# An order written out by hand, products shared between two engines: polysketch attention with a tanh-shrink FFN on Trainium2

## The chip, the cores and the metric

The kernel runs on one core of one Trainium2 chip. The metric is device time in microseconds (us); before the change it is 114.84, the median of three runs (113.99 to 115.63). A core has five engines with a queue each, and each queue runs in its own order: TensorE (PE in the profile; PEld are its weight loads), VectorE (DVE), ScalarE (ACT), GpSimd (POOL) and SyncE (SP), which here only issues DMAs. Queues wait for one another by semaphores.

## The reference

Four batches of four heads, 1088 tokens, head size 32, sketch size r = 8. All inputs and the output are float32.

```python
def phi(x):                                   # 32 -> 8 x 8 = 64 features
    a = np.einsum('rd,bhsd->bhsr', S1, x)
    b = np.einsum('rd,bhsd->bhsr', S2, x)
    return np.einsum('bhsi,bhsj->bhsij', a, b).reshape(*x.shape[:-1], r * r)
q_p, k_p = phi(q), phi(k)
kv  = np.einsum('bhsf,bhsd->bhfd', k_p, v)
z   = np.sum(k_p, axis=2)
num = np.einsum('bhsf,bhfd->bhsd', q_p, kv)
den = np.einsum('bhsf,bhf->bhs', q_p, z)[..., None] + 1e-06
x   = num / den                               # heads side by side: 4352 tokens x 128
h   = x @ w_in                                # 128 -> 2048
out = (h - np.tanh(h)) @ w_out                # 2048 -> 128
```

## The kernel before

**Attention, per batch.** k is transposed on VectorE (`kT`, L583), sketched with S1 and S2 on TensorE (`ksk`, L599, L610), and the sketches are transposed back (`abk`, L616). Three outer products of 768 elements on VectorE make the 64 features of the keys (`w`, L659). TensorE multiplies them with v in 128x32 tiles (L671, `kvmm`). The denominator goes another way: the 8x8 Gram matrix of the two sketches (L638), copied (`gm`, L642), times S2 (L625, `scmm`) gives a third 8-column sketch, so that the product of a query's first and third sketch, summed, is the denominator. The copied kv matrix is transposed (L703) and copied (`kvb`). The queries are transposed (`qT`, L592), sketched in 32x32 tiles (L724), transposed back (`abc`, L729); then VectorE does m = first times third sketch (L741), its sum (L744), 1/den (L747), the first sketch times 1/den (`ap`, L749; called aq in op names), outer products of up to 768 elements (`qp`, L767) and their transposes (`qpT`, L772). The numerator (`num`, L783) is 16 small tiles at a time, 32x32, over the blocks of 128 tokens of a piece. Two casts per piece put it as bf16 into `xT` (L375). A batch has 9 blocks (the last one is half full). Batch 0 is done in pieces of blocks 0 to 2, 2 to 5, 5 to 9; batch 1 in 0 to 5 and 5 to 9; batches 2 and 3 whole.

**FFN.** The 4352 columns of `xT` are taken in ten groups: 256, 384, 448, six of 512, 192. Each has 16 tiles: h = w_in tile times xT (L877), th = -tanh(h) (L881, ScalarE, bf16) and the sum over tiles of w_out tile times th (L892). What is missing, h itself through w_out, comes as two correction matmuls with the product w_in w_out, split into a bf16 high and low part `wch`, `wcl` (L896), over all columns of the group. That product is made on the chip from transposed weights (L845, L855). h lies in one of three PSUM banks; the last three groups, when attention has left its four banks, take pairs of banks and one tanh for 1024 columns. There are 20 tanh tiles of 512 columns. A group ends with a transpose (`ot`, L901) and four stores by SP (eight where a group spans two batches, L911).

**What sets the order.** The kernel makes a list of operations with their reads and writes and with durations and a key; `schedule` runs through them with these durations and appends to each engine's queue the ready operation that can start first, by key within a short window. It also chooses the buffer of each value, and puts filler matmuls (L435: 256 columns of zeros) on TensorE where the plan has it empty in the start. `sync` then sets the semaphores that the dependences need, `emit` issues each queue. GpSimd does memsets, masks and some weight casts; all two-input products but one (`s2r`, L559) are VectorE's. A load waits until at most 1.4 MB of loads are under way. All of k, q, v and the weights are loaded by SP, in order of the keys.

Of the kernel before, what the change touches and what calls it, by code (L numbers as in the profile page):

```python
# [18 lines left out]
GCOLS = [256, 384, 448] + [512] * 6 + [192]  # L19
T_FIRST = 12500.0  # L20
PERIOD = 8900.0
FILL = (214.0, 60.0)
CAP = 1.4e6
PAIRS = 7
URGENT = (-60500.0, 450.0)
PIECES = {0: [(0, 2), (2, 5), (5, 9)], 1: [(0, 5), (5, 9)], 2: [(0, 9)], 3: [(0, 9)]}
OFF = [[0, 9], [17, 26]]
WINDOW = {"tensor": 60.0, "vector": 150.0, "scalar": 60.0, "gpsimd": 30.0, "sync": 30.0}


class _Bank:
    __slots__ = ("t", "ops")

    def __init__(self):
        self.t, self.ops = 0.0, []
# [51 lines left out]
class _Op:  # L87
    __slots__ = ("engs", "fn", "key", "deps", "users", "nleft", "vals", "eng", "lat", "mode",
                 "t0", "t1", "seq", "known", "waits", "inc", "cnt", "sem", "dma", "name", "filler")


class _Prog:
    SWITCH = 125.0
# [4 lines left out]
    def add(self, engs, fn, r=(), w=(), key=0.0, chain=None, dma=0, name="", after=(), mode=None):  # L98
        o = _Op()
        o.engs = engs  # L100
        o.fn, o.key, o.dma, o.name, o.mode = fn, key, dma, name, mode
        o.deps, o.users, o.vals = {}, [], []
        o.filler = False
# [31 lines left out]
    @staticmethod  # L135
    def pick(grp, t):
        best = None
        for c in grp.pool.choices:
            a = 0.0
            for bank in c[0]:  # L140
                if bank.t is None:
                    break
                a = max(a, bank.t)
            else:
                if a <= t and grp.pool.psum:
                    return t, c
                if best is None or a < best[0]:
                    best = (a, c)
        return best and (max(t, best[0]), best[1])

    def schedule(self, filler=None):
        for o in self.ops:
            o.nleft = len(o.deps)
            for d in o.deps:
                d.users.append(o)
            o.t1 = None
        ready = [o for o in self.ops if o.nleft == 0]
        free = {"tensor": 1100.0, "vector": 900.0, "scalar": 900.0, "gpsimd": 900.0, "sync": 700.0}
        self.order = {e: [] for e in free}
        wire = 0.0  # L160
        pemode = None
        fills = True

        def start_of(o, e):
            t = free[e]
            for d, raw in o.deps.items():
                if d.eng == e and not d.dma and e == "tensor":
                    continue
                if d.eng == e and not d.dma:
                    if raw:  # L170
                        t = max(t, d.t1 + d.lat - 45.0)
                    continue
                t = max(t, d.t1 + (0.0 if d.dma else d.lat))
            for v in o.vals:
                if v.grp is not None and v.grp.ap is None:
                    best = self.pick(v.grp, t)
                    if best is None:
                        return None
                    t = best[0]
            return t  # L180

        n = 0
        while n < len(self.ops):
            best = None
            for e in free:
                cands = []
                for o in ready:
                    if e in o.engs:
                        t = start_of(o, e)
                        if t is not None:  # L190
                            cands.append((t, o))
                if not cands:
                    continue
                t0 = min(t for t, _ in cands)
                t, o = min(((t, o) for t, o in cands if t <= t0 + (URGENT[1] if o.key < URGENT[0] and not o.dma else WINDOW[e])), key=lambda x: (x[1].key, x[0]))
                rank = (t, o.key, o.engs[e][0])
                if best is None or rank < best[0]:
                    best = (rank, t, o, e)
            assert best is not None, "stuck"
            _, t, o, e = best  # L200
            for v in o.vals:
                g = v.grp
                if g is not None:
                    if g.ap is None:
                        _, c = self.pick(g, t)
                        g.ap = c[1]
                        m = len(c[0]) // len(g.vals)
                        for u in g.vals:
                            u.banks = c[0][u.index * m:(u.index + 1) * m]
                            u._ap = c[1][u.index]  # L210
                            u.first_deps = [d for bank in u.banks for d in bank.ops]
                            for bank in u.banks:
                                bank.t = None
                    if o in v.phases[0][2]:
                        for d in v.first_deps:
                            o.deps.setdefault(d, d.eng == e and d.seq == len(self.order[e]) - 1)
            if e == "tensor":
                if o.name == "o0.0":
                    fills = False
# [771 lines left out]
```

## Time and profile before

| what | value |
|---|---|
| median of three runs | 114.84 us |
| span of the profiled execution | 112.6 us |
| profiled execution's own time | not listed; the median lies 2.2 us over the span |
| PE busy, instructions | 100.3 us, 1467 |
| DVE busy | 72.1 us, 115 |
| ACT busy | 79.9 us, 164 |
| POOL busy | 5.6 us, 25 |
| first FFN matmul (L877) starts | 19.7 us |
| last output transpose (L901) starts | 108.9 us |
| HBM read, written | 8.81 MB, 2.23 MB |

Busy time is the time in which an engine has an instruction running. Matmuls are pipelined and their ends are modelled, so a row's length (0.38 us for 512 columns) is not what it holds the queue for; the distance from one start to the next is (0.2155 us). A busy PE can still have short holes. The chain is followed back from the last instruction: at each step to what released it. Times in the timeline are from the start of the span.

### The profile page before, as it was taken

The numbers are of one execution on the slowest core, as the hardware profiler recorded it, in microseconds if no ns is written. First come the engines' busy times: TensorE is split into PE (matmuls) and PEld (weight loads), VectorE is DVE, ScalarE is ACT, GpSimd is POOL, SyncE is SP. The second block draws the span as 40 slices with busy tenths as digits, with TensorE's granted clock in tenths as the row PEclk, the third lists the DMA queues.
The fourth block names the chain that finished last, engine by engine and source line by source line (L and its number), as shares of the span: only waits on it lengthen the run. The fifth ranks groups of instructions, "written<-read, shape, count | busy, mean of one in ns | idle before, by whom it ended". The sixth has DMA issues, their size and how long they took to land.

```text
span 112.6 us, 3409 instructions
## 1 busy us (share of the span) xinstructions
PE 100.3 (89%) x1467; PEld 48.7 (43%) x1477; DVE 72.1 (64%) x115; ACT 79.9 (71%) x164; POOL 5.6 (5%) x25
## 2 busy tenths in 40 slices
PE   6975996998799989979999999979999999999960
PEld 4523783455355444436443346334243334334540
DVE  4469374899999999999999992499950020020030
ACT  2101247876487798586599867798969999999950
POOL 5202016000000000000000000000000000000000
PEclk9999999999999999999999999999999999999999
DMA  1999878799987804022000230005004106005035
GB/s 21 259 245 329 255 232 234 243 241 272 226 270 218 165 5 69 0 47 46 0 6 0 44 49 6 6 11 83 0 6 68 25 0 93 0 12 77 4 55 73
DMA packets 25037, 11.24 MB, mean 100 GB/s; under 512 B 18880, under 2 KB 23616, under 8 KB 25024
## 3 DMA queue, kind: packets, MB, share of 16 engines
q1 hardware_dynamic: 24320, 10.97, 40.7%
q8 instruction: 11, 0.18, 0.7%
q10 hardware_dynamic: 704, 0.08, 0.5%
q14 instruction: 2, 0.02, 0.1%
HBM read 8.81 MB, written 2.23 MB: 98 GB/s over the span
## 4 chain that ended last, share of the span: by engine, by line
PE 36%; ACT 28%; DVE 16%; DMA 13%; issue 2%; SPq 1%; DVEq 0%
ACT th L881 25%; PE psb L892 11%; PE psb L877 10%; DMA qL<-in_q_dram 5%; DMA wo_f<-in_moe_w_out_dram 5%; PE psb L783 5%; DVE qp L767 4%; DVE qpT L772 4%; DVE abc L729 3%; DMA kL<-in_k_dram 3%; PE psb L724 3%; PE psb L671 3%; DVE ot L901 2%; PE psb L610 2%; ACT wiT L375 2%
## 5 line engine op out<-in xcount | busy, mean ns | idle before, releaser
L881 ACT ACTIVATE th<-psb 128x512 bf16<-128x512 f32 (+4 forms) x136 | 69.5, 624 | 7.4 <-PE psb L877 6.6
L877 PE MATMUL psb<-xT,wi 128*128 128x512 bf16 (+4 forms) x155 | 50.1, 349 | 1.5 <-DVE xT L375 0.5
L892 PE MATMUL psb<-th,wo 128*128 128x512 bf16 (+4 forms) x157 | 48.2, 348 | 1.4 <-DVE ot L901 0.6
L877 PEld LDWEIGHTS psb<-xT,wi 128*128 128x128 bf16 x160 | 14.9, 97 | 25.3 <-ACT th L881 14.4
L892 PEld LDWEIGHTS psb<-th,wo 128*128 128x128 bf16 x160 | 14.6, 97 | 15.7 <-ACT th L881 7.5
L901 DVE STREAM_TRANSPOSE ot<-psb 128x512 f32<-128x512 f32 (+4 forms) x10 | 6.3, 626 | 22.6 <-PE psb L892 22.6
L772 DVE STREAM_TRANSPOSE qpT<-qp 128x768 f32<-128x768 f32 (+1 forms) x14 | 12.1, 861 | 0.4
L767 DVE TENSOR_TENSOR qp<-ap,abc 128x768 f32<-128x768 f32 (+1 forms) x14 | 11.5, 818 | 0.1
L659 DVE TENSOR_TENSOR w<-abk 128x768 f32<-128x768 f32 x12 | 11.3, 981 | 0.1
L729 DVE STREAM_TRANSPOSE abc<-psb 128x1152 f32<-128x1152 f32 (+2 forms) x5 | 5.7, 1143 | 5.1 <-PE psb L724 5.0
L435 PE MATMUL psb<-zz 128*128 128x256 bf16 x33 | 7.8, 388 | 1.1 <-DVE zz L434 1.1
L783 PE MATMUL psb<-qpT,kvb 32*32 32x128 f32 (+4 forms) x448 | 8.3, 309 | 0.1
L375 ACT CAST xT<-psb 128x192 bf16<-128x192 f32 (+4 forms) x8 | 3.3, 421 | 5.4 <-PE psb L783 5.4
L583 DVE STREAM_TRANSPOSE kT<-kL 128x576 f32<-128x576 f32 (+1 forms) x8 | 5.6, 724 | 1.7 <-DMA kL<-in_k_dram 1.7
L783 PEld LDWEIGHTS psb<-qpT,kvb 32*32 32x32 f32 x448 | 5.1, 103 | 2.9 <-DVE qpT L772 2.0
L671 PE MATMUL psb<-w,vL 128*32 128x64 f32 x288 | 6.0, 243 | 0.0
L592 DVE STREAM_TRANSPOSE qT<-qL 128x1088 f32<-128x1088 f32 (+2 forms) x5 | 5.3, 1055 | 0.9 <-DMA qL<-in_q_dram 0.9
L435 PEld LDWEIGHTS psb<-zz 128*128 128x128 bf16 x33 | 4.1, 135 | 3.6 <-DVE zz L434 1.1
L671 PEld LDWEIGHTS psb<-w,vL 128*32 128x32 f32 x288 | 5.1, 125 | 0.3 <-issue 0.2
L642 ACT COPY gm<-psb 128x32 f32<-128x32 f32 x4 | 0.8, 198 | 5.6 <-PE psb L638 5.6
L724 PE MATMUL psb<-qT,wq 32*32 32x288 f32 (+2 forms) x160 | 3.6, 381 | 0.9 <-ACT xT L375 0.9
L375 DVE CAST xT<-psb 128x192 bf16<-128x192 f32 (+3 forms) x6 | 2.8, 467 | 1.1 <-PE psb L783 1.0
(55 smaller groups left out, 56.6 us busy)
## 6 DMA issues: line engine op xcount, KB each, us to landing
kL<-in_k_dram SPq DMA_DIRECT2D x3, 544.0 KB, 3.6
qL<-in_q_dram SPq DMA_DIRECT2D x3, 544.0 KB, 4.9
vL<-in_v_dram SPq DMA_DIRECT2D x4, 288.0 KB, 4.8
vL<-in_v_dram SPq DMA_DIRECT2D x4, 256.0 KB, 5.0
wi_f<-in_moe_w_in_dram SPq DMA_DIRECT2D x4, 256.0 KB, 4.7
wo_f<-in_moe_w_out_dram SPq DMA_DIRECT2D x4, 256.0 KB, 5.8
out_dram<-ot SPq DMA_DIRECT2D x16, 64.0 KB, 2.0
out_dram<-ot SPq DMA_DIRECT2D x8, 56.0 KB, 1.9
```

The lines of the kernel that those rows point to most:

```text
L375: return e.copy(o, i) if name == "scalar" else e.tensor_copy(o, i)
L435: filler = (lambda e, n: e.matmul(bank(3)[:, 0:256], zz.ap[:, 0:128], zz.ap[:, 128:384], start=True, stop=True), zop)
L659: P.add(_v(768), lambda e, n: e.tensor_tensor(out=wv.ap.rearrange("p (x i j) -> p x i j", i=8, j=8), in0=abh(0)[:, :, :, None].to_broadcas ...
L671: i = e.matmul(pv[b].ap[h * 32:(h + 1) * 32, 0:64], vL[b][:, h, blk * 32:(blk + 1) * 32], wvs[b, p].ap[:, (bi * 4 + h) * 64:(bi * 4 + h + ...
L729: P.add(_vp(sn * 4), lambda e, n: e.transpose(abc.ap.rearrange("p k h f -> p h k f")[:, :, 0:s1 - s0, :], psa4[:, :, 0:sn].rearrange("p h ...
L767: P.add(_v(cn * 256), lambda e, n, qp=qp, c0=c0, cn=cn: e.tensor_tensor(out=qp.ap[:, 0:cn * 256].rearrange("p (x i j) -> p x i j", i=8, j= ...
L772: P.add(_v(cn * 256), lambda e, n, qp=qp, o0=o0, cn=cn: e.transpose(qt.ap[:, o0 * 256:(o0 + cn) * 256], qp.ap[:, 0:cn * 256]), r=[qp], w=[ ...
L783: i = e.matmul(psa4[h * 32:(h + 1) * 32, g, 0:nb * 32], kvb.ap[g * 32:(g + 1) * 32, x, h * 32:(h + 1) * 32], qq[g * 32:(g + 1) * 32, 0:nb, ...
L877: P.add(_pe(n_ / 2.4 + 2.6), lambda e, n, jb=jb, hv=hv: e.matmul(hv.ap[:, jb % m * 512:jb % m * 512 + n_], wi[jb // 4].ap[:, (jb % 4) * 12 ...
L881: P.add(_a(n_ * m), lambda e, n, hv=hv, th=th: e.activation(out=th.ap.rearrange("p (u x) -> p u x", u=m)[:, :, 0:n_], in_=hv.ap.rearrange( ...
L892: fn = lambda e, n, x=x, st=st, sp_=sp_: e.matmul(ov.ap[:, 0:n_], wo[x // 4].ap[:, x % 4, :], ths[x][0].ap[:, ths[x][1] * 512:ths[x][1] * ...
L901: P.add(_vp(n_), lambda e, n: e.transpose(ot.ap[:, 0:n_], ov.ap[:, 0:n_]), r=[ov], w=[ot], key=-60000, name=f"ot{gi}")
```

## The change

`schedule` with its durations and keys goes. In its place a table, worked out beforehand, lists every operation in one sequence: its number, the engine that takes it (v, a, g, t, s), and the index of the buffer that it takes where it is the first to use one; F and f are fillers of 512 and 256 columns. The table starts with (numbers 66, 67: the keys' sketch; 70: Gram; 75 to 77: outer products; 84: sketch of the first 384 queries)

```
0v 52g 16s 15a 1g 54g 18s 2g 12g 17s 3g 19s 7g 10g 13g 30s 22s 29s 62v:0 20s 4v 5v 23s 63v 61g 50v 64v 21s 51v F F F F
F F F F F F 66t:0 65v 24s 6v 67t 60g 53g 8g 9g 68v:0 25s 69v f F F F F 70t:0 83v 76g:0 26s 71a:0 f F 72t 103v 27s 73a
14g 74v 56g F F F 84t:0 75v:1 35s 107t:0 77g:2 85v:0 78t:1 79t 108v:1 86g:0 F 80t 109g:1 34s 225a 87v:0 88v:0 f F
```

What else it does:

- Two-input operations on VectorE and all such on GpSimd are marked `lock`: each waits for the last marked one on the other engine, so that a product on one never runs beside a product on the other. With that, GpSimd takes w0.1, w0.2, w1.0, w2.0 to w2.2, w3.0, w3.1, most m, some aq, and all qp but that of the first 384 tokens. Number 75 (w0.0) stands behind 74 on VectorE, and 77 (w0.2, GpSimd) behind 75.
- The first 384 tokens of batch 0 are sketched by one full 128x128 matmul with a block-diagonal matrix (`wqd`), one product of 768 elements, and one numerator of two full matmuls against a block-diagonal kv (`kvd0`, made by a transpose of kv on VectorE, the head transpose `kvh`, and a masked product on GpSimd). The rest of batch 0 is one piece of six blocks, batch 1 one piece of nine.
- k is loaded and, in batch 0, transposed and sketched in other halves; v is loaded by heads, q in two parts. A load waits until at most 1.45 MB are under way. The loads of batch 3 reuse buffers of batch 0.
- Groups are 384, 352, 352 (batch 0 exactly), six of 512, 192. In groups 5 to 8 VectorE adds h to th for the first 192 or 320 columns of each tile (`dg`, out of the PSUM bank of h), and the correction matmuls leave these columns out.
- 36 tanh tiles: 16 of them lie in the float32 weight buffers, once the weights are cast.
- The scale matmul is one for batches 1 to 3, with a masked sum on VectorE (`scx`, `sc`); the k-v products of a batch are three operations that other work may come between; weight transposes and products are in blocks of four.
- An operation on VectorE, ScalarE or GpSimd now waits also for earlier ones of its own engine that it must not overtake (before: only where it reads their result).

```diff
-GCOLS = [256, 384, 448] + [512] * 6 + [192]
...
+GCOLS = [384, 352, 352] + [512] * 6 + [192]
+CAP = 1.45e6
 PAIRS = 7
...
+GDIR = {5: 192, 6: 320, 7: 320, 8: 320}
+CUT0 = [0, 12, 34]
+PIECES = {0: [(3, 9)], 1: [(0, 9)], 2: [(0, 9)], 3: [(0, 9)]}
...
+    def plan(self, table, filler):
...
+            if o.lock and e in lastl:
+                d = lastl["gpsimd" if e == "vector" else "vector"]
+                if d is not None:
+                    o.deps.setdefault(d, False)
+                lastl[e] = o
+            o.eng, o.at, o.seq = e, at, len(self.order[e])
...
-                            if d.eng == e and not (raw and e != "tensor"):
+                            if d.eng == e == "tensor":
...
-        P.add(_v(768), lambda e, n: e.tensor_tensor(
+        P.add({**_v(768), **_gt(768)}, lambda e, n: e.tensor_tensor(
             out=wv.ap.rearrange("p (x i j) -> p x i j", i=8, j=8),
...
+    def q_heads(i):
+        c0, c1, (_, ) = qvals[0][i]
+        nx = c1 - c0
+        q_transpose(0, i)
...
+        P.add(_pe(70 + nx * 53.3, 230.0), lambda e, n: e.matmul(
+            pq.ap[:, 0:nx * 32], wqd.rearrange("p h f -> p (h f)"), qt_.ap, start=True, stop=True),
+            r=[qt_, wqds, wqdc], w=[pq], mode="128x128", name=f"qsk0.{i}")
...
+            for x in range(2):
+                r = e.matmul(pn.ap[:, 0:nx * 32], kvd0.ap[:, x, :], qq[:, :, x, :], start=(x == 0), stop=(x == 1))
+            return r
+        P.add(_pe(100 + nx * 106.7, 175.0), num, r=[kvd0, qt], w=[pn], mode="128x128", name=f"num0.{i}")
...
+                if gc:
+                    P.add(_vp(gc * m), lambda e, n, hv=hv, th=th: e.tensor_tensor(
+                        out=th.ap.rearrange("p (u x) -> p u x", u=m)[:, :, 0:gc],
+                        in0=hv.ap.rearrange("p (u x) -> p u x", u=m)[:, :, 0:gc],
+                        in1=th.ap.rearrange("p (u x) -> p u x", u=m)[:, :, 0:gc], op=ALU.add),
+                        r=[hv, th], w=[th], name=f"dg{gi}.{jb // m}", lock=True, after=[act])
...
-                    ov.ap[:, 0:n_], x.ap[:, :], xt, start=st, stop=sp_)
+                    ov.ap[:, gc:n_], x.ap[:, :], xt[:, gc:n_], start=st, stop=sp_, skip_group_check=bool(gc))
```

760 lines of the change are left out of this document (382 added, 378 removed).

## The prediction

> **What bounds the kernel now.** I read the page's 40 slices first, then the chain in order of time, then the timeline of the first 32 us and the weight loads by stage.
>
> ```profile
> PE   6975996998799989979999999979999999999960
> DVE  4469374899999999999999992499950020020030
> ACT  2101247876487798586599867798969999999950
> POOL 5202016000000000000000000000000000000000
> DMA  1999878799987804022000230005004106005035
> ```
>
> One slice is 2.8 us. TensorE is busy from slice 8 to slice 39. VectorE is full from slice 9 to 27 and nearly free after it, GpSimd idle after slice 7, and the DMA engines are full to slice 12. The chain, in order of time (start, length, what):
>
> ```profile
> 16.96 1.83 ACT wiT L375 x2
> 18.79 0.18 ACT xT L375
> 19.10 0.81 PE psb L724 x32
> ...
> 47.01 0.71 DVE qpT L772
> 47.72 0.44 DVE xT L375
> ...
> 84.43 20.98 ACT th L881 x28
> ...
> 108.89 0.38 DVE ot L901
> ```
>
> So there are three stretches: a start until the first FFN matmul at 19.7 us, a long middle in which TensorE is the limit with holes where VectorE's products are late (the chain runs through VectorE from 39.5 to 47.7), and an end from 84.4 in which tanh is.
>
> The ledger of TensorE from 19.7 to 108.9 (89.2 us): FFN matmuls of 512 columns start 0.2155 us apart, so 0.42 ns a column; 34 matmuls (16 h, 16 o, 2 correction) on 4352 columns are **62.3**. The attention pieces and the 16 small weight products, each from its start to the next FFN matmul's start, add to **20.2**. That leaves **6.6** empty, which by stage (weight loads counted, times their step) are 1.2 (19.7 to 24.7), 1.4 (to 31.4), 0 (to 37.3), 1.5 (to 51.3), 0.8 (to 66), 0.1 (to 84.2) and 1.6 (to the end). After 108.9 come the last transpose, stores and end: 3.7. Sum 19.7 + 89.2 + 3.7 = 112.6, the span. The profiled execution's own time is not listed; the median of the three runs is 2.2 over its span, and I carry that 2.2. The three runs spread by 1.4%; some 2% is what a measurement of this kernel can tell from no change.
>
> **The start.** The new order on VectorE begins as the old one did: the first half of k lands at 4.2, then four transposes (0.43 and 0.37 each in place of 0.78 and 0.70), two masks, the sketch matrix. The keys' sketch is transposed by about 8.25, against 8.13 now. Two things then differ: 12 products go partly to GpSimd, and the fillers ahead of each TensorE piece are twice as long (512 columns).
>
> ```profile
> L435 PE MATMUL psb<-zz x7: 421/421/421, 3.7 to 4.9; 128*128 128x256 bf16 x7
> ...
> L435 PE MATMUL psb<-zz x5: 272/273/421, 16.2 to 16.8; 128*128 128x256 bf16 x5
> ```
>
> These two answers for one line show the same filler at two times (min/median/max ns). The page's granted clock reads 1.00 throughout, and yet the filler takes 421 ns, 0.223 apart, up to 16 us, and 272 from there on. At the slow rate a 512-column filler holds the queue for 0.43, at the fast one for 0.21.
>
> ```profile
> 4.44 0.40 POOL L559 TENSOR_TENSOR s2r<-sin,mask 128x128 f32<-128x128 f32 x1 [2.12 <-DMA sin<-in_S_dram]
> ...
> L556 POOL COPY wq<-stt 128x16 f32<-128x16 f32 x2 | 0.3, 205 | 0.3 <-DVE stt L546 0.3
> L767 DVE TENSOR_TENSOR qp<-ap,abc 128x768 f32<-128x768 f32 x8 | 7.5, 938 | 0.1
> ```
>
> A product of 768 elements takes 0.94 on VectorE. GpSimd has none. Below: at the slope of its one-input rows (512 elements 613 ns, 16 elements 205: 0.82 ns each) 0.82 us. Above: the only two-input row, 128 elements in 400 ns, with no fixed part, 2.4. I take the line through that row and the copy of 16 (1.74 ns an element): **1.5**, since it is the same operation with the same broadcast. The Trainium skill (GPSIMD Engine Reference, 3.1) measures 4497 ns for 2048 elements, 1.96 times VectorE, and its section 4.1 says to use VectorE for elementwise work; scaled, that is an estimate of 1.69 us, by which the sum below would be 1.3 more. No run so far shows it.
>
> Now the chain to the first FFN matmul, with TensorE turning fast around 10.5 (it is nearly always busy from 6.2 on). Sketch ends 7.2; one short and four long fillers behind it, slow, hold the Gram matmuls to 9.1 (they run at 8.2 now); copy, two fillers, the scale matmuls and their two copies: 10.8. Behind that copy on VectorE waits w0.0, which also waits for w0.1 on GpSimd (8.3 to 9.8): 10.8 to 11.8. Then w0.2 on GpSimd, which waits for w0.0: 11.8 to 13.4. In that time VectorE transposes abc for the 384 and the 768 tokens (0.5 and 1.0). m0.0 and m0.3 on GpSimd (0.3 and 0.5): 14.3. den, ap on VectorE, the head transpose: 15.1. The 768-element product for 384 tokens 16.1, 1/den for the others 16.4, transpose 17.4. The numerator, two full 4-byte matmuls of 384 columns: 1.4 (two 128-column transposes in the same type hold the queue for 0.38), 18.8. Two copies on ScalarE (0.32 each): 19.5; the three fillers meanwhile hide. First FFN matmul: **19.8**, against 19.7. The weights do not hold it: by bytes wi3 lands near 14.5 as now, its cast and transposes end by 15.8. If TensorE stays slow to 16 as now, about 21.0; if it is fast from 5.5, 18.7. So the start is a wash, but it delivers 384 tokens, not 256.
>
> **The FFN stretch.** (a) Rest of batch 0: two numerators (0.9 and 1.17) become one of six blocks; between the rows of five and nine blocks below, 1.35 with its switch: -0.7.
>
> ```profile
> 46.45 1.17 PE L783 MATMUL psb<-qpT,kvb 32*32 32x160 f32 x64
> ...
> 82.04 1.60 PE L783 MATMUL psb<-qpT,kvb 32*32 32x288 f32 x64
> ```
>
> (b) Batch 1: 1.20 and 1.25 become one 9-block numerator of 1.76: -0.7. (c) Groups 5 to 8 subtract tanh directly on VectorE for 192, 320, 320 and 320 columns, and the two correction matmuls leave these out: 1152 x 2 x 0.42 ns = -0.97. (d) Two of the k-v products are split by other work, the scale matmul stands apart, a sketch loses its neighbour. Each entry into small tiles and back idles about 0.16 twice: +1.65, less 0.35 for fewer scale matmuls: +1.3. (e) The added subtractions: 40 on VectorE at 0.3 to 0.75, some 23 us, in the slices where it reads 0 to 2; nothing is queued behind them but output transposes. But each holds its PSUM bank until it is done. With three banks a round is h 0.38 + tanh 0.63 + subtraction 0.42 + about 0.2 of handing over = 1.63, 0.54 a tile against tanh's 0.49; TensorE has 0.45 of FFN plus 2 to 3 us of attention per group there, so I charge 0.3 in all; without that cover it would be 32 x 0.05 = 1.6.
>
> (f) The empty time. The 256-column group goes, in which tanh at 0.28 a tile outlasted TensorE's 0.22, and the wait for the second numerator: 2.6 becomes 0.8. The batch-1 chain is what is late next. Counted from the first FFN matmul: TensorE has 21.4 us of work ahead of batch 1's numerator. GpSimd has four casts, w1.0, w2.0, m1 and three products: ksk2 at 9.9, its transposes 10.9, w2.0 12.4, abc1 and m1 14, den, 1/den, scale and ap on VectorE 16.3, products 17.8, 19.3 and 20.8, transposes (abc2 of batch 2 lies between them) 22.5. So 1.2, plus 0.6 for the copies before group 3. Batches 2 and 3 have 8 us to spare. The end keeps 0.9 of its 1.6, since 36 tanh tiles in place of 20 let h run further ahead. With the 0.3: **3.8** empty. What is saved by fewer waits on VectorE costs waits between VectorE and GpSimd: each product waits for the last one on the other engine, with transposes, reductions and copies queued behind it, and TensorE behind these.
>
> Sum: 62.3 - 0.97 + 20.2 - 0.1 + 3.8 = 85.2. With 19.8 and 3.7: span **108.7**, plus 2.2: **110.9**, 3.4% less. The loads are more and smaller (SP pays 0.34 or 0.62 each), and the last of batch 2's v queues behind two stores that wait for the first output at 34; it is wanted near 49, so nothing.
>
> **Rivals.** (1) **Products on GpSimd are the new bound.** If one takes p, 2.4 products' worth lies on the start (w0.1, w0.2, the two m) and 4.4 on the batch-1 chain (w2.0, m1, three products): 108.7 + 6.8 (p - 1.5). It decides against the change from p = 2.07, and at the upper bound of 2.4 it gives 114.8 + 2.2 = 117.0, 2% slower. For it: the single two-input row has no second point. Against: the copy row fixes the overhead. 0.16. (2) **The fast clock comes early.** Fillers from 1.1 to 5.4, then hardly a hole: the start 18.7, and 2.3 empty in place of 3.8: 106.1 + 2.2 = 108.3; with products at 0.82 the start loses 1.4 more and the batch-1 hole of 1.2 closes: 105.7. The Trainium skill (TensorE: Matmul & The Clock Gate, Part 1) has the array fast after about 3.4 us of sustained work, in windows whose phase varies by run. By that rule this rival holds; the trace agrees only in part, as 4.05 us of fillers without a hole left the filler at 421 ns at 7.2. 0.22. (3) **The written order does not fit the chip**, each queue waits at other places than planned and the empty time stays at 6.6, with a slow start at 21.0: 21.0 + 88.0 + 3.7 + 2.2 = 114.9, no change. For it: five queues in a fixed order, where one late member stops all. Against: 36 tiles of slack. 0.18. The forecast itself: 0.44, by itself 109.2 to 112.5.
>
> **Numbers.** Faster: the forecast, rival 2, little else: 0.66. Same: rival 3 and the milder part of rival 1: 0.20. Slower: 0.14. The range takes in rivals 2 and 3 and half of rival 1: 105.0 to 116.0.
>
> **What would show it.** First FFN matmul at 19.8; filler spacing near 10 us; a 768-element GpSimd product at 1.5; batch 1's numerator 22.5 us behind the first FFN matmul; last o matmul 85 behind it. I am wrong if GpSimd rows are above 2 us, if the first FFN matmul is past 21.5, or if TensorE shows holes in groups 5 to 8 behind the subtractions.

## The result, and the profile after

The kernel after took **105.25 us** (median of four runs, 104.97 to 107.3), the kernel before 114.41 beside it: a ratio of 0.919, 95% interval 0.912 to 0.925. A second set of six runs, with experiments between, gave 0.930 (0.925 to 0.935). The change makes the kernel 7 to 8% faster; 3.4% was forecast. The profiled execution took 105.29, its span is 103.5.

The slices of the kernel after, in the same form as those of before (a slice is 2.6 us now):

```profile
PE   5999969999999999999999989999999999999920
DVE  0577898619958899229798897687888789999310
ACT  4001596997799896999897789999969999999810
POOL 5135849870063998999303960000000000000000
```

TensorE reads 9 from slice 1 to 37, but for one 6 and one 8; before, it had 5 to 8 in five of the first ten slices and 7 or 8 in four later ones. GpSimd works up to slice 23. VectorE is loaded evenly to the end, where it was full from 8 to 28, but for slices 24 and 25, and then nearly idle. The chain of the kernel after, in order of time (start, length, what), a few of its links:

```profile
7.50 1.53 POOL w L642
9.31 0.88 DVE w L642
10.26 1.52 POOL w L642
...
99.14 0.38 DVE ot L947
```

The start runs through products that go from GpSimd to VectorE and back, as the prediction laid it out; the last output transpose starts at 99.1, where it was 108.9. What TensorE waited for, after the opening (engine, line, releaser: us in total, times, longest):

```profile
PE psb L731 <- DVE qpT L724: 0.9, 1, 0.9
PE psb L938 <- DVE th L926: 0.4, 1, 0.4
PE psb L917 <- ACT wi_f L921: 0.2, 1, 0.2
PE psb L917 <- ACT gm L617: 0.2, 1, 0.2
PE psb L917 <- DVE wi_f L926: 0.2, 1, 0.2
PE psb L938 <- issue: 0.2, 1, 0.2
PE psb L917 <- issue: 0.2, 1, 0.2
```

The first line is the last wait before the first FFN matmul. The six others, 1.4 us together, are all that the view names behind it; none is for a query product (`qpT`) or for `xT`. Each of the six stands right behind an attention piece, so the ledger below, in which a piece lasts up to the next FFN matmul, has them in the pieces. Put into the prediction's own ledger of TensorE, made in the same way:

| us | before | forecast | measured |
|---|---|---|---|
| up to the first FFN matmul | 19.7 | 19.8 | 17.7 |
| FFN and correction matmuls | 62.3 | 61.3 | 61.5 |
| attention pieces, weight products | 20.2 | 20.1 | 18.3 |
| empty | 6.6 | 3.8 | 1.6 |
| end | 3.7 | 3.7 | 4.4 |
| span | 112.6 | 108.7 | 103.5 |

So of the 5.2 us by which the span was missed, 2.1 lie in the start and 4.0 in the attention pieces and the empty time; the end gave 0.7 back and the columns 0.2. The ledger reads a single stretch to some 0.3 us, since a piece is counted up to the next FFN matmul. Where pieces and empty time of further kernels are told below, all are counted in one way, up to the start of the last o matmul: 20.0 and 6.4 for the kernel before, 18.3 and 1.3 for the kernel after.

One thing in these profiles belongs to no part of the change. In twelve of the eighteen experiments TensorE stands still once between 25 and 34 us for 0.25 to 2.2 us, often amid the matmuls of one group, and the profile names nothing that it waited for ("issue"); the longest are 2.2 in e13, 1.8 in e2, 1.6 in e10, 1.3 in e14, 1.2 in e9 and 0.9 in e8. The two kernels as first profiled, e1, e4, e5, e6, e12 and e17 have no such hole there. Its cause is open, and it goes into the pieces and empty time of those runs.

### The profile page after: what moved, and what is told of

It reads as the page before. It is cut to its first block, busy times and chain, and to the rows that moved or that the text cites. A ratio compares the mean times of both kernels' runs of the same rounds, so it can differ in the third digit from the quotient of the medians.

```text
span 103.5 us, 3024 instructions
## 1 busy us (share of the span) xinstructions
PE 95.5 (92%) x1244; PEld 47.8 (46%) x1253; DVE 75.7 (73%) x137; ACT 80.4 (78%) x161; POOL 38.5 (37%) x56
## 4 chain that ended last, share of the span: by engine, by line
PE 70%; DVE 12%; POOL 7%; ACT 4%; issue 2%; DVEq 0%
PE psb L938 25%; PE psb L917 24%; PE psb L429 5%; PE psb L813 4%; PE psb L579 3%; ACT wi_f L921 3%; POOL w L642 3%; POOL qp L797 3%; PE psb L942 2%; DVE w L642 2%; DVE ot L947 2%; PE psb L731 2%; PE psb L754 1%; DVE abc L759 1%; PE psb L657 1%
## 5 line engine op out<-in xcount | busy, mean ns | idle before, releaser
L917 PE MATMUL psb<-xT,wi 128*128 128x512 bf16 (+3 forms) x153 | 46.4, 347 | 0.7 <-ACT wi_f L921 0.2
L921 ACT ACTIVATE th<-psb 128x512 bf16<-128x512 f32 (+3 forms) x81 | 42.9, 600 | 2.2 <-PE psb L917 2.1
L938 PE MATMUL psb<-th,wo 128*128 128x512 bf16 (+3 forms) x95 | 26.8, 339 | 0.1
L797 POOL TENSOR_TENSOR qp<-ap,abc 128x768 f32<-128x768 f32 x11 | 16.4, 1511 | 3.1 <-DVE ap L779 3.0
L921 ACT ACTIVATE wo_f<-psb 128x512 bf16<-128x512 f32 (+3 forms) x27 | 15.3, 612 | 2.1 <-PE psb L813 1.1
L921 ACT ACTIVATE wi_f<-psb 128x512 bf16<-128x512 f32 (+2 forms) x28 | 15.4, 623 | 0.9 <-PE psb L917 0.6
L926 DVE TENSOR_TENSOR th<-psb,th 128x192 bf16<-128x192 f32 (+2 forms) x26 | 13.9, 541 | 3.0 <-ACT th L921 1.9
L642 POOL TENSOR_TENSOR w<-abk 128x768 f32<-128x768 f32 x8 | 12.1, 1515 | 7.9 <-DVE abk L590 6.8
L802 DVE STREAM_TRANSPOSE qpT<-qp 128x768 f32<-128x768 f32 x11 | 10.5, 958 | 0.9 <-POOL qp L797 0.9
L938 PE MATMUL psb<-wo_f,wo 128*128 128x512 bf16 (+2 forms) x31 | 10.3, 353 | 0.5 <-DVE th L926 0.4
```

The costliest lines, as they stand in the source:

```text
L642: P.add({**_v(768), **_gt(768)}, lambda e, n: e.tensor_tensor(out=wv.ap.rearrange("p (x i j) -> p x i j", i=8, j=8), in0=abh(0)[:, :, :, N ...
L797: P.add({**_v(cn * 256), **_gt(cn * 256)}, lambda e, n, qp=qp, c0=c0, cn=cn: e.tensor_tensor(out=qp.ap[:, 0:cn * 256].rearrange("p (x i j) ...
L802: P.add(_v(cn * 256), lambda e, n, qp=qp, o0=o0, cn=cn: e.transpose(qt.ap[:, o0 * 256:(o0 + cn) * 256], qp.ap[:, 0:cn * 256]), r=[qp], w=[ ...
L917: P.add(_mm(n_), lambda e, n, jb=jb, hv=hv: e.matmul(hv.ap[:, jb % m * 512:jb % m * 512 + n_], wi[jb // 4].ap[:, (jb % 4) * 128:(jb % 4 + ...
L921: act = P.add(_a(n_ * m), lambda e, n, hv=hv, th=th: e.activation(out=th.ap.rearrange("p (u x) -> p u x", u=m)[:, :, 0:n_], in_=hv.ap.rear ...
L926: P.add(_vp(gc * m), lambda e, n, hv=hv, th=th: e.tensor_tensor(out=th.ap.rearrange("p (u x) -> p u x", u=m)[:, :, 0:gc], in0=hv.ap.rearra ...
```

## The start: when the array turns fast

The filler's line tells the rate again. TensorE in the kernel after (start, length, what, number):

```profile
1.12 4.45 PE L429 MATMUL psb<-zz 128*128 128x512 bf16 x10 [1.12 <-DVE zz L427]
...
6.52 1.03 PE L429 MATMUL psb<-zz 128*128 128x512 bf16 x4
...
17.67 0.66 PE L917 MATMUL psb<-xT,wi 128*128 128x384 bf16 x3
```

Ten fillers take 4.45 us at the opening, 0.43 each; four take 1.03 at 6.5, which is three steps of 0.2155 and the last one's 0.38. The array is fast from about 5.4, not from 10.5 as the forecast had it.

**Half of the opening fillers.** e1 takes five of the ten out of the table:

```diff
-... 21s 51v F F F F F F F F F F 66t:0 65v ...
+... 21s 51v F F F F F 66t:0 65v ...
```

> The changed kernel with five of the ten opening fillers, so that TensorE is empty from about 3.3 us to the keys' sketch at 5.5; nothing else differs. Theory A (the fast clock comes early because TensorE has no hole from 1.1 us on): the filler behind the sketch takes 634 ns and starts 0.43 apart, the first FFN matmul comes at 19 to 20 in place of 17.7, the time is 1.5 to 2.5 us over 105.25. Rival (the clock turns by a phase of its own, whatever is queued): filler at 379 ns, first FFN matmul at 17.7, 105.3 again.

Measured: 107.75 us (107.11 to 109.23), ratio 0.945 (0.938 to 0.952). Its TensorE:

```profile
6.89 1.91 PE L429 MATMUL psb<-zz 128*128 128x512 bf16 x4
...
19.56 0.66 PE L917 MATMUL psb<-xT,wi 128*128 128x384 bf16 x3
```

The same four fillers behind the sketch take 1.91, the Gram matmuls and the sketch of the queries come late in their turn, and the first FFN matmul starts 1.9 later. Behind it nothing changes: 18.3 us of pieces and 1.3 empty. The start that the forecast took for the kernel after, fast near 10.5 and first FFN matmul at 19.8, is this one: its fillers at 10.2 still start 0.40 to 0.43 apart, and the matmuls from 12 on are fast. The early clock is worth some 2 us: 1.9 in the traces, 1.7 to 3.0 by the ratios, against 0.930 and 0.919 for the kernel after. It is the ten fillers that bring it.

**More fillers in the kernel before.** e5 puts four more in front of the first sketch (23 of 256 columns, in place of 19):

```diff
+        more = 0 if self.order["tensor"] else 4
-        while t + FILL[0] + FILL[1] < b:
+        while t + FILL[0] + FILL[1] < b + more * FILL[0]:
```

> The kernel before with four more opening fillers (23 of 256 columns), so that TensorE has no hole between 1.1 us and the keys' sketch at 6.0. Theory A: the fast clock comes with it, the filler behind the sketch takes 272 ns in place of 421, and the small pieces of the start shorten by some 1.5 us in all; as loads and copies also bound that start, the first FFN matmul comes 0.4 to 1.2 earlier than 19.7 and the time is 113.2 to 114. Rival (the clock has its own phase): filler at 421, time as before.

Measured: 113.77 (113.18 to 115.62), ratio 0.996 (0.991 to 1.000), a gain of 0.5 us (0 to 1.0). The array was fast from 3.7, and the first FFN matmul came 0.9 earlier than in the profile of before. In the trace this reaches the end: the last o matmul starts at 107.6 in place of 108.6, and pieces and empty time together are the same, 26.3 against 26.4 (7.7 of it empty in place of 6.4). The ratio shows less of it. It compares with runs of the kernel before of which some had the early clock too, as the next paragraph shows, so it doesn't settle what the clock is worth there. Nor did the clock stay: the filler at 13.4 took 0.42 again, and those from 14.9 on 0.27.

**How sure the early clock is.** The fillers behind the first sketch can be read in every profile. In all eleven of the written order with ten opening fillers the four of 512 columns took 1.03, and every later filler was fast. With the kernel before's opening (19 of 256) the three of 256 took 0.50 in four profiles and 0.82 in three, the one that the prediction read among them. One of these three, e17, had been fast: its last opening fillers start 0.11 apart, those behind the sketch 0.19 and 0.21. The four that were fast behind the sketch didn't stay so either: single fillers between 8 and 14 us took 0.39 to 0.42 again. In the kernel before's opening there are holes between the pieces of the start; in the written order fillers stand in most of them. The Trainium skill (TensorE: Matmul & The Clock Gate, Part 1) has the array fast once a window of about 3.4 us, which runs free of the kernel, was busy, so that the moment varies from run to run. These profiles agree: 19 fillers, 4.24 us where all of them are slow, with a hole behind them, catch it in some runs; ten of 512 columns, up to 4.45 us, with the sketch at once behind them, caught it in all. The prediction read one profile, in which 4.05 us of fillers left the array slow, and took it for the rule; it was one draw.

## The middle: products on two engines

Where the products ran, and how long one took (line, engine, operation, tile, count, then busy us, mean ns, idle before), in the kernel after:

```profile
L797 POOL TENSOR_TENSOR qp<-ap,abc 128x768 f32<-128x768 f32 x11 | 16.4, 1511 | 3.1 <-DVE ap L779 3.0
L642 POOL TENSOR_TENSOR w<-abk 128x768 f32<-128x768 f32 x8 | 12.1, 1515 | 7.9 <-DVE abk L590 6.8 <-DVE w L642 1.1
```

The price of 1.5 us, taken from a line through two rows of the trace of before, was right. Now the busy times by stretch of time, of the kernel before and then of the kernel after (window, its length, then PE, PEld, DVE, ACT, POOL busy; clock, DMA share, GB/s):

```profile
19.70:40.00 20.30, 19.16 (x393) 10.14 (x383) 19.40 (x31) 14.40 (x42) 0.00 (x0) 1.00 0.84 227
40.00:62.00 22.00, 20.34 (x359) 9.46 (x361) 21.34 (x32) 17.25 (x41) 0.00 (x0) 1.00 0.13 22
```

```profile
17.70:40.00 22.30, 22.27 (x415) 11.85 (x421) 17.32 (x28) 19.80 (x54) 13.63 (x16) 1.00 0.77 223
40.00:62.00 22.00, 21.01 (x355) 10.78 (x358) 16.32 (x29) 19.09 (x39) 15.09 (x13) 1.00 0.11 19
```

VectorE was busy for 40.7 of 42.3 us. After, it is busy for 33.6 of 44.3, with 28.7 on GpSimd; in 19.5 us of these both work at once (added up from the intervals in the trace). The two-input products exclude each other by their waits; what runs beside a product on GpSimd is a transpose on VectorE, more rarely a copy out of PSUM or a reduction.

**All products on VectorE.** e2 gives the 27 two-input operations that the table has on GpSimd back to VectorE, each in its place of the sequence.

```diff
-76g:0 ... 77g:2 ... 86g:0 ... 109g:1 ... 82g ... 112g:1 ... 113g:1 ... 115g:2 ... 130g:3 ...
+76v:0 ... 77v:2 ... 86v:0 ... 109v:1 ... 82v ... 112v:1 ... 113v:1 ... 115v:2 ... 130v:3 ...
```

> The changed kernel's order with all 27 shared products on VectorE, at the same places of the order. Theory B (the holes of the middle went because GpSimd takes products off VectorE's chain): VectorE gets 8 x 0.9 + 11 x 0.92 + 8 small ones, some 21 us more on 76, is full to the end and bounds the kernel: 110 to 114 us, TensorE's empty time 6 us or more. Rival (the written order and the fewer pieces closed the holes, the products' place is worth little): under 107.

Measured: 115.09 (114.33 to 115.53), ratio 1.010 (1.004 to 1.017): the whole gain is gone. The first FFN matmul comes 0.9 later, and pieces and empty time together are 29.5 us (1.8 of it the hole without a named wait), where the kernel after has 19.6. VectorE is busy for 93.3 us.

**The same without the direct subtraction**, so that VectorE has about the work of the kernel before (68.3 us busy in its profile; 72.1 there): e8 is e2 with this besides (groups 5 to 8 then have their correction matmuls over all columns, and these additions leave the table):

```diff
-GDIR = {5: 192, 6: 320, 7: 320, 8: 320}
+GDIR = {}
```

> The changed kernel's order with all products on VectorE and without the direct subtraction: VectorE has 71 us of work, as in the kernel before (72), so this is the written order and the fewer pieces alone. Theory B (sharing is what closed the holes): empty time of 4 us or more in the middle, 109 to 111. Rival (the order did): 106.2 to 107, which is 105.3 and the 0.97 of the correction columns.

Measured: 115.36 (113.81 to 116.04), ratio 1.001 (0.996 to 1.005). The written order, the larger pieces and the early clock gain nothing when VectorE has the products. The order was laid out for sharing, so this does not say what an order laid out for VectorE alone would do.

**Sharing in batches 2 and 3 only.** e18 moves 11 operations of batches 0 and 1 back to VectorE, 8 of them of 768 elements; 16 stay on GpSimd, 11 of that size (not 13, as the expectation says).

```diff
-76g:0 ... 77g:2 ... 86g:0 ... 109g:1 ... 112g:1 ... 113g:1 ... 115g:2 ...
+76v:0 ... 77v:2 ... 86v:0 ... 109v:1 ... 112v:1 ... 113v:1 ... 115v:2 ...
```

> The kernel after, with the 11 operations of batches 0 and 1 that it has on GpSimd (3 key products, 5 query products, m and the scale) on VectorE in the same places of the order; batches 2 and 3 still share. If the sharing earns its place at the start and in batch 1's chain, as the prediction had it, most of the 10 us goes: 111 to 114 us. If it is batches 2 and 3, where 13 shared products lie, less than half goes: 106 to 109.

Measured: 110.85 (110.16 to 111.81), ratio 0.970 (0.963 to 0.977). A half of what sharing is worth sits in the start and in batch 1's chain, a half in batches 2 and 3: the result falls between the two ranges. The numerator of batch 1 shows the first half; here it is in the kernel after, in e18 and in e2:

```profile
39.17 1.60 PE L813 MATMUL psb<-qpT,kvb 32*32 32x288 f32 x64
```

```profile
43.84 1.60 PE L813 MATMUL psb<-qpT,kvb 32*32 32x288 f32 x64 [1.20 <-DVE qpT L802]
```

```profile
45.65 1.60 PE L813 MATMUL psb<-qpT,kvb 32*32 32x288 f32 x64 [1.56 <-DVE qpT L802]
```

**One numerator in batch 1, in the kernel before.** e6:

```diff
-PIECES = {0: [(0, 2), (2, 5), (5, 9)], 1: [(0, 5), (5, 9)], 2: [(0, 9)], 3: [(0, 9)]}
+PIECES = {0: [(0, 2), (2, 5), (5, 9)], 1: [(0, 9)], 2: [(0, 9)], 3: [(0, 9)]}
```

> The kernel before with batch 1 in one numerator of nine blocks, all else by its planner. By the rows 0.8 us of TensorE goes (1.11 and 1.23 become 1.54): 113.6. Rival: the numerator now waits for all three products on VectorE's chain, which is what the middle waits for, and group 3 starts later: 115 to 116, the part alone is a loss.

Measured: 119.29 (118.82 to 119.68), ratio 1.045 (1.040 to 1.051). With a full VectorE the one numerator comes at 49.1 and TensorE waits for it:

```profile
49.10 2.59 PE L783 MATMUL psb<-qpT,kvb 32*32 32x288 f32 x64 [2.62 <-DVE qpT L772]
```

So a part that was priced at -0.7, as matmul time saved, costs 5 us alone, and in the kernel after nothing waits for it. Its price depends on who makes the products.

**Sharing without the written order.** e9 lets the planner of the kernel before put products on either engine, at 1.51 us on GpSimd; e10 does this with one numerator in batch 1.

```diff
+def _gt(n):
+    return {"gpsimd": (n * 1.81 + 120.0, 150.0)}
...
-        P.add(_v(768), lambda e, n: e.tensor_tensor(
+        P.add({**_v(768), **_gt(768)}, lambda e, n: e.tensor_tensor(
...
-            P.add(_v(cn * 256), lambda e, n, qp=qp, c0=c0, cn=cn: e.tensor_tensor(
+            P.add({**_v(cn * 256), **_gt(cn * 256)}, lambda e, n, qp=qp, c0=c0, cn=cn: e.tensor_tensor(
```

> The kernel before with its own planner, groups and pieces; only the 768-element products of keys and queries may also go to GpSimd, priced 1.51 us there, and the planner puts 5 of 12 key products and 9 of the query products on it. No operation is locked. If the sharing alone is what the change lives on, VectorE falls from 72 to some 60 us busy, the 6.6 us of empty TensorE time before fall below 4 and the time is 107 to 111 us. If the sharing needs the written order (products side by side on both engines lengthen each other, and the planner does not know it), the empty time stays above 6 and the time is 113 or more.

> As the one with shared products and the kernel before's planner, but batch 1 is one numerator of nine blocks. Alone, the one numerator made the kernel before 4.5% slower, because VectorE brought its products late. If that late VectorE was the reason, shared products take the loss back: within 1.5 us of the version with shared products alone (the numerator itself is worth -0.7). If the one piece is bad in itself, it is again some 5 us above that version.

Measured: e9 116.08 (115.56 to 117.1), ratio 1.021 (1.015 to 1.028); e10 116.71 (116.42 to 117.42), ratio 1.027 (1.021 to 1.032). In e9 the planner puts 14 products on GpSimd, some 12 us of VectorE's time; VectorE is busy for only 7.6 us less, and the kernel is not faster but slower. The key products that e9 shares between GpSimd and VectorE:

```profile
L663 POOL TENSOR_TENSOR w<-abk 128x768 f32<-128x768 f32 x5 | 10.6, 2128 | 19.2 <-DVE abk L620 19.2
L663 DVE TENSOR_TENSOR w<-abk 128x768 f32<-128x768 f32 x7 | 10.4, 1519 | 0.1
```

One takes 2128 ns in the mean on GpSimd and 1519 on VectorE, where the planner reckons with 1.51 us on GpSimd and where one took 981 ns on VectorE in the kernel before. Three of them, two on VectorE and one on GpSimd, begun together at 28.1, take 3.14 us; three in a row on VectorE alone took 2.69 in e6. This is why sharing gains little here; that e9 is slower than before is not shown to come from it alone, as e9 has the 1.2 us hole without a named wait as well. What e10 does say is that the loss of e6 is no matter of the piece alone: with shared products one numerator costs 0.6 us, which is within the spread, not 5.

**Sharing one at a time, without the written order.** e13 chooses 13 products for GpSimd and adds the wait of the kernel after to the planner, which reckons with it; batch 1 is one numerator. e14 has the same order without the waits (the line `o.deps.setdefault(d, False)` goes). e17 is e13 again, in more rounds, as the first runs spread too far for a ratio.

```diff
+            if locked(o, e) and lastl[other[e]] is not None:
+                d = lastl[other[e]]
+                t = max(t, d.t1 + d.lat)
...
+            if locked(o, e):
+                d = lastl[other[e]]
+                if d is not None:
+                    o.deps.setdefault(d, False)
+                lastl[e] = o
```

> The kernel before with its planner, groups and fillers; batch 1 is one numerator; 13 chosen products (2 of the first 3 query products' kind in batch 0, 3 in batch 1, 4 in batches 2 and 3, and 4 key products) go to GpSimd, and each two-input product waits for the last one on the other engine, which the planner reckons with. If sharing one at a time is enough, the 6.6 us of empty TensorE time fall to about 3 and the time is 108.5 to 111 us (the planner's own sum falls by 3.9 against the kernel before). If it takes the written order, it stays at 113 or more, near the freely shared version's 116.7.

> The same order and the same 13 products on GpSimd, but the waits between the engines' products are left out. If the wait protects both engines, products that meet lengthen (GpSimd rows at 2 us and more, VectorE rows at 1.5) and the time is 2 us or more above the version with the waits. If it only costs its handing over, the time is the same or up to 1 us less, as it was within 1% in the kernel after without its waits.

> The planner's order with 13 shared products, one at a time, and one numerator in batch 1, once more. If sharing one at a time needs the written order, 112 to 115 us, a ratio of 0.98 to 1.01. If the first runs were a disturbed chip, 108.5 to 111.

Measured: e13 114.94 (112.37 to 116.7); e17 114.09 (112.9 to 116.17), ratio 0.996 (0.992 to 1.000); e14 114.86 (112.84 to 116.51), ratio 0.994 (0.988 to 0.999). VectorE is down to 59 us of work and TensorE still waits: in e17 3.0 us for one transpose of key sketches and 1.9 for one of k. Sharing by itself, with the wait or without it, is worth about half a per cent (at most 1.2 by the intervals) in this planner's order. The two together make the gain: pieces and empty time are 26.4 us in the kernel before, 28.1 in e8 with the order alone, 24.9 in e17 with the sharing alone (27.9 in e13, the same kernel, 2.2 of it the hole without a named wait), 19.6 in the kernel after. What is called the order here is the whole rest of the change, with its larger pieces, loads and fillers, and e17 shares 13 operations, not 27; which of these count, the runs do not separate. A planner that looks further ahead might do better with the same sharing.

**The wait itself.** In e13 and then e14, the key products on either engine (e17 has 1516 and 954 ns, as e13):

```profile
L680 POOL TENSOR_TENSOR w<-abk 128x768 f32<-128x768 f32 x4 | 6.1, 1515 | 14.6 <-DVE w L680 14.6
...
L680 DVE TENSOR_TENSOR w<-abk 128x768 f32<-128x768 f32 x8 | 7.4, 953 | 0.1
```

```profile
L680 POOL TENSOR_TENSOR w<-abk 128x768 f32<-128x768 f32 x4 | 7.6, 1900 | 10.9 <-DVE abk L637 10.9
...
L680 DVE TENSOR_TENSOR w<-abk 128x768 f32<-128x768 f32 x8 | 10.0, 1283 | 0.1
```

Without the wait both rows lengthen by about what they overlap, and the time is the same. e7 takes the waits out of the kernel after and keeps its order:

```diff
-            if o.lock and e in lastl:
+            if False and e in lastl:
```

> The changed kernel without the waits that keep the products of VectorE and GpSimd apart; the order in each queue and all data waits stay. If the products get in one another's way on the chip, their rows lengthen where they meet (GpSimd's 1.51 to 2 us or more, VectorE's 0.92 up to 1.5) and the time is 105.3 to 107; if they do not, waits go and it is 104.5 to 105.3.

Measured: 106.08 (105.53 to 107.27), ratio 0.928 (0.922 to 0.933), the same as with them. Only where products meet do they lengthen: the four key products on VectorE from 950 to 1261 ns in the mean, the masked product of kv on GpSimd from 612 to 1237. The Trainium skill (SBUF — State Buffer, SBUF: two separate sides) says that VectorE, where both inputs lie in SBUF, and GpSimd take one pair of ports by an exclusive lock, for the whole instruction. The rows agree with it: in e9 the GpSimd product that began together with one on VectorE took 2.28 us, near the sum of both alone (0.94 and 1.51). So the chip holds one product back by itself, and a semaphore in front of it only makes the order certain. What is left as the reason is that the order puts a transpose, not a product, beside each product; this is argued from what runs side by side, and no run changes it alone.

## The end, and two versions meant to be faster

**No direct subtraction**: e3, the same edit of `GDIR` in the kernel after.

> The changed kernel without the direct subtraction in groups 5 to 8: the correction matmuls cover all columns. By columns TensorE gets 1152 x 2 x 0.42 ns = 0.97 us more where it is full, so 106.2. If the subtraction's hold on the PSUM banks or its place in VectorE's queue costs time, under 105.3; if tanh is the bound there, 105.3.

Measured: 106.3 (105.5 to 107.28), ratio 0.931 (0.925 to 0.938). The kernel after had 0.919 and 0.930, so the times do not tell whether the subtraction gains anything. Counted by columns the FFN takes 62.5 in place of 61.5; in the traces, from the first FFN matmul to the last o matmul, 82.7 us against 81.2 and 81.9 (e12). That fits the step that was priced at 0.97, but the profiled run of e3 was its slowest, 107.28.

**Twenty tanh tiles** in place of 36, in the same order, each tile the one longest free: e4. Of its edit, the line that takes the tiles away:

```diff
-    th_p = _Pool([([tb[i]], [ths_[i // 2][:, i % 2 * 512:i % 2 * 512 + 512]]) for i in range(NTH + 16)])
+    th_p = _Pool([([tb[i]], [ths_[i // 2][:, i % 2 * 512:i % 2 * 512 + 512]]) for i in range(NTH)])
```

> The changed kernel with 20 tanh tiles in place of 36, each taken by the longest free; the order is unchanged, since no more than 19 tiles are alive at any place of it. The prediction's step (h runs further ahead with 36 tiles, 0.7 us at the end): about 106. Rival (the order itself sets how far h runs ahead, the tiles add nothing): 105.3.

Measured: 105.61 (105.05 to 107.17), ratio 0.926 (0.920 to 0.932): no change. On every engine the instructions come in the same order as in the kernel after, with 20 tiles as with 36.

**Two moves.** By the ledger two things looked too dear in the kernel after: on VectorE the head transpose of kv and the 1/den of the other tokens stand ahead of the product that starts the first numerator (0.4 us), and the k-v products of batches 2 and 3 are split (two more entries into small tiles). e11 moves both, e15 the first alone, e16 the second alone, e12 is the kernel after beside e11.

```diff
 on VectorE                        (e11, e15)
-den0.0 ... kvh den0.3 rd0.3 qp0.0 qpT0.0
+den0.0 ... qp0.0 kvh qpT0.0 den0.3 rd0.3
 on TensorE                        (e11, e16)
-kvmm2.0 ... kvmm2.1    kvmm3.0 kvmm3.1 ... kvmm3.2
+kvmm2.0 kvmm2.1        kvmm3.0 kvmm3.1 kvmm3.2
```

> The kernel after with two moves in the table: on VectorE the head transpose of kv and the 1/den of the other tokens go behind the product and the transpose of the first 384 tokens, and two k-v products of batches 2 and 3 go back to the rest of their batch. By the ledger the start gains 0.4 us and two entries into small tiles fewer gain 0.6: 104.3 to 104.8 us against 105.3. If the first numerator then waits for the masked kv product instead, and the splits were hidden, the time is 105.3 again.

> The kernel after, unchanged, beside the others on one chip: 105.3 us by its first run (104.97 to 107.3). It gives the bound of what two versions of it can be told apart by.

> The kernel after, with the head transpose of kv and the 1/den of the other tokens moved behind the product of the first 384 tokens and its transpose on VectorE, and nothing else. If this move is what lost 1.7 us in the version with both moves, it is 107 to 108 us; if the k-v products were, it is 105.0 to 105.7 (the numerator starts 0.4 earlier).

> The kernel after, with the split k-v products of batches 2 and 3 put back together, and nothing else. If together they are cheaper (two entries into small tiles fewer), 105.0 to 105.7 us. If it is they that lost the 1.7 us, because TensorE then waits for the last key product in one place or starves tanh for longer, it is 107 to 108.

Measured: e11 107.68 (106.98 to 108.34), ratio 0.945 (0.940 to 0.950), beside e12 with 106.0 (104.93 to 106.35), ratio 0.930; e15 106.69 (105.49 to 108.88), ratio 0.930 (0.922 to 0.938); e16 106.85 (105.78 to 107.77), ratio 0.930 (0.923 to 0.938). Neither move gains, and both together lose 1.7 us. TensorE in the kernel after (e12) and in e16, at the same point of the order:

```profile
61.41 0.88 PE L657 MATMUL psb<-w,vL 128*32 128x64 f32 x48
62.66 0.38 PE L938 MATMUL psb<-wo_f,wo 128*128 128x512 bf16 x1 [0.37 <-DVE th L926]
```

```profile
61.62 0.59 PE L917 MATMUL psb<-xT,wi 128*128 128x512 bf16 x2
63.17 0.39 PE L917 MATMUL psb<-xT,wi 128*128 128x512 bf16 x1 [0.95 <-DVE th L926]
```

There VectorE has a 0.98 transpose of query products and an output transpose of 0.67 ahead of the first subtractions, and the next h waits for a PSUM bank. The split k-v product lies in that hole; put elsewhere, it leaves 0.95 open, in e16 and in e11 alike. In e15 the first numerator waits 0.4 instead of 0.8, as meant, but a weight cast on GpSimd, behind the masked product of kv that was moved with it, then comes 0.7 late:

```profile
PE psb L938 <- POOL wo L359: 0.7, 1, 0.7
```

The profiles of e11, e15 and e16 also have the hole without a named wait, 0.5, 0.7 and 0.5 us in the midst of a sketch of queries, which e12 has not. So a part of what these versions lose in their profiles is not shown to come from the moves. Why the two moves cost more together than apart was not followed further.

## Why the direction was right and the size wrong

Right:

- The price of a GpSimd product: 1.5 forecast, 1.51 measured. Rival 1, with products at 2.07 or more, is out.
- The numerators (-0.7 and -0.7 forecast; -0.7 and -0.8) and, within what the ledger can read, the other pieces, in which the split k-v products lie (+1.3; some +1.1). The correction columns (-0.97) hold by count; the times of e3 can't confirm them.

That 105.25 lies between 105.0 and 116.0 is luck. The lower end stood for rival 2 with products at 0.82 us (105.7), and they took 1.51.

Wrong, by the prediction's own steps:

- **"With TensorE turning fast around 10.5"** in the step on the start: it was 5.4. Rival 2, with 0.22, is what happened in the start. Its 18.7 for the first FFN matmul was still 1.0 too late; its condition, "fillers from 1.1 to 5.4, then hardly a hole", was the right one. e1 restores the forecast's clock, and its 19.56 is the forecast's 19.8 but for 0.2; w0.0 starts at 10.6 (10.8 forecast), w0.2 ends at 13.2 (13.4), the transpose ends at 17.2 (17.4): the chain was worked out correctly, on the wrong clock. Term mis-sized: 2.1 us.
- **"20.2 - 0.1"** for the small work. Each piece of before was measured from its start to the next FFN matmul, so that it held waiting. The 16 weight products took 1.74 so, and 0.90 in the kernel after for the same matmuls (220 and 219 ns each); a filler that the ledger of before has among the pieces went too (0.42). Waits that the change could take away stood in the ledger as work. Of the 1.8 us this explains 1.3; the rest is spread over the other pieces.
- **(f), 3.8 empty.** 1.6 is left. The 1.8 charged to batch 1's chain, 1.2 and 0.6 for the copies, is not there: its numerator was to start 22.5 us behind the first FFN matmul and started 21.5 behind it, level with TensorE's 21.4 us of work ahead, and between 29 and 42.5 us the view of waits names none. What the ledger still has empty there, some 0.8, are steps of 352 columns that here and there stand 0.16 to 0.20 apart, a few more, in place of 0.15. The stretch behind the last numerator, charged 0.9, keeps some 0.3; it does so with 20 tanh tiles (e4) and without the subtractions (e3) too, so the argument that 36 tiles would help the end fell, and what closed it is open. The subtractions were miscounted, 48 and not 40, and are 26.1 us of VectorE's time, not 23; TensorE shows one wait for them that is longer than the 0.16 behind other pieces (0.37), so 0.3 was enough. And "what is saved by fewer waits on VectorE costs waits between VectorE and GpSimd" was wrong in kind: in this order TensorE waits for hardly any of them. 2.2 us.
- The end took 4.4, not 3.7, and the time over the span was 1.8, not 2.2. No run went after either.

Rival 3, the written order that does not fit the chip, did not come. The forecast named the parts and priced them one by one; e2, e6, e8, e9 and e17 show that in the middle these parts have no price of their own. The order without the sharing: nothing. The sharing without the order: half a per cent or a loss. One numerator: 5 us lost alone.

## What to carry to other kernels

VectorE, at 96% in the stretch that sets the pace, was relieved by a second engine where the order lays work of another kind beside what the two can't do at once; moving products alone gained next to nothing here, and moving them back out of the order made for it cost 9 to 10 us. When a time is read off as work, from one start to the next, look for the waits inside it first. A state that one profile shows, such as a clock that turned late, is one draw: put its other outcome into the sum with more than a small chance.

## What the runs showed of the hardware

- The moment at which TensorE first turned fast ran from 3.7 us (e5) to 16 us (the kernel before); in the latter the clock's row reads 1.00 throughout. The length of the fillers showed the rate, the row did not.
- A start that has turned fast can turn slow again, and then the row does fall. Its slices go down to 0.5 in e5, e6, e10, e13, e14 and e17, which were fast by 7 us and slow again by 14; it is 0.83 in the mean over the first 19.7 us of e13. The 256-column fillers of e13 took 0.50 for three at 6.7, one took 0.39 at 8.1, and two took 0.63 at 12.1. In the kernel before and in e9, slow from the first filler, the row stays at 1.00.
- Two-input products on VectorE and GpSimd hold each other up, by close to a whole instruction where they begin together (612 to 1237 ns for one; in the mean of groups 1515 to 1900 and 953 to 1283), while transposes on VectorE and a GpSimd product leave each other alone: 1511 and 1515 ns over the 19 products, and a transpose of 768 query features takes 958 ns in the kernel after, 973 in the kernel before.
